# Two attention heads per pass, and later expert weight loads, in a fused attention and mixture-of-experts kernel

## The chip, the cores and the metric

One core of one Trainium2 chip. The metric is device time in microseconds (us). Executions of one kernel agree within about 0.3%, so a per cent is well resolved, except where a run is said to scatter. All runs below gave correct results and count as fast ones.

The engines are PE (matmuls and transposes; its weight loads are listed as PEld), DVE (vector), ACT (activations and copies), POOL (here it mainly issues DMAs) and SP (issues DMAs). PSUM is the memory in which the kernel collects PE's results. A head is one (b, h) pair; a pass of the changed kernel is one turn of its loop, with two heads.

## The reference, cut to what matters

```python
B, H, S, Ns, D = 8, 8, 512, 32, 64            # attention: 64 heads (b, h)
scores = (x @ state.T) / sqrt(D)              # 512 x 32 for each head
xread  = softmax_rows(scores) @ state         # "reads of x":     512 x 64
sread  = softmax_rows(scores.T) @ x           # "reads of state":  32 x 64
x = concatenate([xread, sread])               # 4352 tokens x 512
P = exp(x @ w_gate - max)                     # router logits, 8 experts
for _ in range(8):                            # normalisation (Sinkhorn)
    P /= P.sum(1); P /= P.sum(0); P *= N / E
out = sum(P[:, e:e+1] * (relu(x @ w1[e]) @ w2[e]) for e in range(8))
```

## The kernel before

The attention loop handles one head at a time:

```python
mwp = tile_pool("moe_w", bufs=2); gps = tile_pool("gate_psum", bufs=1, PSUM)
for e in range(E):                       # expert weights, first thing
    nc.gpsimd.dma_start(out=w1e, ...); nc.gpsimd.dma_start(out=w2e, ...)
# ... transposed state stT_all for all heads ...
for bh in range(NH):                     # 64 heads
    nc.sync.dma_start(out=x_nat, in_=x[b, h]...)          # 128 x (4*64), f32
    nc.vector.tensor_copy(out=x_natb, in_=x_nat)          # bf16
    for c in range(4):
        nc.tensor.transpose(xT_ps[:, c, :], x_nat[:, c, :], identf)   # x transposes
    nc.scalar.copy(out=xT, in_=xT_ps)                     # to bf16
    nc.tensor.matmul(esc_ps, sT, xT)                      # scores, 32 x 512
    nc.scalar.activation(out=esc, in_=esc_ps, func=Exp, scale=SCALE, accum_out=rs2)
    for c in range(4): nc.tensor.transpose(eT_ps[:, c, :], esc[:, ts(c, P)], ...)
    nc.vector.tensor_copy(out=eT, in_=eT_ps)
    for c in range(4): nc.tensor.matmul(xr_ps[:, c, :], esc[:, ts(c, P)], s1)   # 65 columns: reads and row sum
    nc.vector.reciprocal(rs1, xr_ps[:, :, D])
    # ... four scalings of 64 columns, two on ACT and two on DVE ...
    for c in range(4): nc.tensor.transpose(xrT_ps[:, c, :], xr[:, c, :], ident)  # read transposes
    for c in range(4): nc.tensor.matmul(sr_ps, eT[:, c, :], x_natb[:, c, :])     # state reads
    # ... scale, transpose, copies into xmT, the transposed tokens ...
for nt in range(34):                     # router logits, 128 tokens each
    # four matmuls of 8 columns into a "gp" PSUM tile, then Exp into Pm
# ... normalisation of Pm on DVE, with one small PE matmul an iteration ...
# ... experts: h = relu(w1.T x), y = w2.T h, acc += Pm * y ...
```

The softmax here doesn't subtract the row's maximum and nothing guards it: scores larger than these inputs give would overflow.

## Time and profile before

| stage (from the timeline) | us |
|---|---|
| until the first scores | 19.4 |
| attention | to 247.9 |
| logits, normalisation, first expert matmuls | to 295 |
| the rest of the experts, output | to 1222.1 |

First the page of the kernel before: span, busy time by engine, then two rows in 40 slices of the span. The digits are tenths, in the first row of busy time and in the second of the clock that was recorded as granted to PE.

```profile
span 1222.1 us, 14811 instructions
PE 1180.9 (97%) x6013; PEld 566.2 (46%) x6104; DVE 337.8 (28%) x804; ACT 472.8 (39%) x1063; POOL 16.2 (1%) x26
...
PE   5999999994999999999999999999999999999998
...
PEclk9999999996999999999999999999999999999999
```

PE is the busy engine. The dip in slice 10 is the normalisation. Groups of instructions of the same kernel follow: line, engine, operation, tiles, shapes, count, then busy us, mean ns of one, idle time before. L114 are x transposes, L152 read transposes, L120 scores, L137 x reads.

```profile
L114 PE MATMUL xT_ps<-identf,x_nat 128*64 128x128 f32 x256 | 83.6, 421 | 11.6 <-DMA x_nat<-in_x_dram 9.6
L152 PE MATMUL xrT_ps<-ident,xr 128*64 128x128 bf16 x256 | 63.7, 312 | 0.5 <-DVE xmT L167 0.3
L120 PE MATMUL esc_ps<-xT,stT_all 64*32 64x512 bf16 x64 | 38.7, 605 | 0.0
L137 PE MATMUL xr_ps<-st_all,esc 32*128 32x65 bf16 x256 | 35.4, 231 | 0.0
```

Matmuls overlap, so these means are latencies. The distance between starts gives PE's real time, and by that measure a head takes 3.56 us (27 heads from 100.4 to 196.6 us). The chain of waits of the kernel before, from 100 to 110 us, is PE alone ("by line" gives shares of the window):

```profile
by line: PE xT_ps L114 34.0%; PE xrT_ps L152 20.3%; PE esc_ps L120 16.1%; PE xr_ps L137 10.4%; PE sr_ps L157 9.8%; PE eT_ps L130 6.5%; PE srT_ps L162 4.8%
```

This is the timeline of PE in the kernel before, where the experts begin: start, us, line, operation, count of matmuls run together.

```profile
250.03 1.01 PE L211 MATMUL h_ps<-xmT,w1e 128*128 128x512 bf16 x2
...
250.99 1.44 PE L211 MATMUL h_ps<-xmT,w1e 128*128 128x512 bf16 x3
...
252.37 1.22 PE L211 MATMUL h_ps<-xmT,w1e 128*128 128x512 bf16 x4
...
254.50 1.02 PE L211 MATMUL h_ps<-xmT,w1e 128*128 128x512 bf16 x4
```

Three 512-column matmuls took 1.44 us at 251 us, and four took 1.02 us at 254.5 us. Within those three the starts lay 0.38 and 0.43 us apart, within the four 0.22 us. PE therefore has two rates here and was at the lower one when attention ended. Scores are also 512 columns wide and took 604 to 606 ns in all 64 heads, against a median of 379 ns in the experts. The Trainium skill, "TensorE: Matmul & The Clock Gate", section "Single matmul latency", gives (219 + N) / 1.2 ns at the low clock and (398 + N) / 2.4 ns at the high one: 609 and 379 for N = 512. This trace agrees with both within 1%, though the page states it for a full array, which these scores (64x32) do not fill. The recorded clock does not show it: it reads 9 or more from the first slice, attention's slices included. The packed trace of this kernel has no clock entry before 252.8 us, where the matmuls get shorter, and the page counts time without an entry as full.

Last, the normalisation in the kernel before: window, its length, then busy us (and instructions) of PE, PEld, DVE, ACT, POOL, the granted clock, the DMA share and GB/s.

```profile
276.00:295.50 19.50, 3.43 (x13) 2.82 (x13) 14.63 (x35) 0.00 (x0) 0.00 (x0) 0.61 0.00 1
```

PE has 3.4 us of work in 19.5 us; DVE works alone.

### The profile page before, as it was taken

The numbers are of one execution on the slowest core, as the hardware profiler recorded it, in microseconds if no ns is written. First come the engines' busy times: TensorE is split into PE (matmuls) and PEld (weight loads), VectorE is DVE, ScalarE is ACT, GpSimd is POOL, SyncE is SP. The second block draws the span as 40 slices with busy tenths as digits, with TensorE's granted clock in tenths as the row PEclk, the third lists the DMA queues.
The fourth block names the chain that finished last, engine by engine and source line by source line (L and its number), as shares of the span: only waits on it lengthen the run. The fifth ranks groups of instructions, "written<-read, shape, count | busy, mean of one in ns | idle before, by whom it ended". The sixth has DMA issues, their size and how long they took to land.

```text
span 1222.1 us, 14811 instructions
## 1 busy us (share of the span) xinstructions
PE 1180.9 (97%) x6013; PEld 566.2 (46%) x6104; DVE 337.8 (28%) x804; ACT 472.8 (39%) x1063; POOL 16.2 (1%) x26
## 2 busy tenths in 40 slices
PE   5999999994999999999999999999999999999998
PEld 3545544542445444544454445444544544454444
DVE  2444443426212122122222112122122222123333
ACT  3555555540333333433333333333433333333332
POOL 2000000000000000000000000000000000000000
PEclk9999999996999999999999999999999999999999
DMA  9211111000001200300040004000400040001112
GB/s 172 56 37 37 39 35 40 14 1 1 1 1 26 44 1 1 56 13 1 1 69 1 1 1 69 1 1 1 69 1 1 1 69 1 1 1 70 69 69 87
DMA packets 53892, 35.31 MB, mean 29 GB/s; under 512 B 37184, under 2 KB 45376, under 8 KB 53824
## 3 DMA queue, kind: packets, MB, share of 16 engines
q0 software_dynamic: 15136, 17.05, 9.6%
q1 hardware_dynamic: 38688, 17.31, 5.1%
q8 instruction: 48, 0.79, 0.3%
q14 instruction: 20, 0.16, 0.1%
HBM read 42.48 MB, written 8.91 MB: 42 GB/s over the span
## 4 chain that ended last, share of the span: by engine, by line
PE 96%; DVE 2%; DMA 1%; issue 1%; ACT 0%; ACTq 0%
PE y_ps L221 38%; PE h_ps L211 38%; PE xT_ps L114 6%; PE xrT_ps L152 4%; PE esc_ps L120 3%; PE xr_ps L137 2%; PE sr_ps L157 2%; DMA x_nat<-in_x_dram 1%; PE eT_ps L130 1%; PE srT_ps L162 1%; DVE ske L186 0%; PE ske_ps L188 0%; PE stT_ps L94 0%; DVE Pm L185 0%; DVE Pm L191 0%
## 5 line engine op out<-in xcount | busy, mean ns | idle before, releaser
L215 ACT ACTIVATE hte<-h_ps 128x512 bf16<-128x512 f32 (+1 forms) x576 | 330.2, 574 | 625.6 <-PE h_ps L211 589.9
L221 PE MATMUL y_ps<-w2e,hte 128*128 128x512 bf16 x2127 | 481.8, 380 | 4.3 <-DVE acc L227 1.6
L211 PE MATMUL h_ps<-xmT,w1e 128*128 128x512 bf16 (+1 forms) x2262 | 482.4, 368 | 2.4 <-issue 0.2
L231 DVE SCALAR_TENSOR_TENSOR acc<-y_ps,Pm,acc 128x512 f32<-128x512 f32 x238 | 178.7, 751 | 628.2 <-PE y_ps L221 627.3
L211 PEld LDWEIGHTS <-w1e 128*128 128x128 bf16 x2304 | 224.5, 98 | 242.7 <-issue 0.6
L221 PEld LDWEIGHTS <-hte 128*128 128x128 bf16 x2176 | 212.9, 98 | 255.6 <-issue 4.7
L114 PE MATMUL xT_ps<-identf,x_nat 128*64 128x128 f32 x256 | 83.6, 421 | 11.6 <-DMA x_nat<-in_x_dram 9.6
L152 PE MATMUL xrT_ps<-ident,xr 128*64 128x128 bf16 x256 | 63.7, 312 | 0.5 <-DVE xmT L167 0.3
L117 ACT CAST xT<-xT_ps 64x512 bf16<-64x512 f32 x64 | 36.7, 574 | 28.9 <-PE xT_ps L114 28.0
L152 PEld LDWEIGHTS <-xr 128*64 128x64 bf16 x256 | 29.5, 139 | 39.2 <-issue 10.6
L227 DVE TENSOR_SCALAR acc<-y_ps,Pm 128x512 f32<-128x512 f32 x34 | 25.3, 750 | 74.7 <-PE y_ps L221 70.2
L114 PEld LDWEIGHTS xT_ps<-identf,x_nat 128*64 128x64 f32 x256 | 30.7, 145 | 28.1 <-issue 10.0
L123 ACT ACTIVATE esc<-esc_ps 32x512 bf16<-32x512 f32 x64 | 37.2, 581 | 14.9 <-PE esc_ps L120 14.8
L167 DVE COPY xmT<-xrT_ps 64x512 bf16<-64x512 bf16 x64 | 26.7, 417 | 58.2 <-PE xrT_ps L152 58.2
L144 ACT ACTIVATE xr<-xr_ps,rs 128x64 bf16<-128x64 f32 x128 | 38.5, 301 | 7.7 <-DVE rs L140 7.2
L120 PE MATMUL esc_ps<-xT,stT_all 64*32 64x512 bf16 x64 | 38.7, 605 | 0.0
L147 DVE TENSOR_SCALAR xr<-xr_ps,rs 128x64 bf16<-128x64 f32 x128 | 34.6, 271 | 14.1 <-ACT xr L144 13.1
L137 PE MATMUL xr_ps<-st_all,esc 32*128 32x65 bf16 x256 | 35.4, 231 | 0.0
L157 PE MATMUL sr_ps<-x_natb,eT 128*32 128x64 bf16 x256 | 27.9, 240 | 0.0
L160 ACT ACTIVATE sr<-sr_ps,r 32x64 bf16<-32x64 f32 x64 | 19.5, 305 | 16.0 <-PE sr_ps L157 15.6
L110 DVE CAST x_natb<-x_nat 128x256 bf16<-128x256 f32 x64 | 18.5, 289 | 19.4 <-PE sr_ps L157 15.1
L169 ACT COPY xmT<-srT_ps 64x32 bf16<-64x32 bf16 x64 | 11.4, 178 | 30.6 <-PE srT_ps L162 30.2
(41 smaller groups left out, 232.4 us busy)
## 6 DMA issues: line engine op xcount, KB each, us to landing
out_dram<-o SPq DMA_DIRECT2D x34, 256.0 KB, 2.0
x_nat<-in_x_dram SPq DMA_DIRECT2D x64, 128.0 KB, 2.2
w1e<-in_moe_w_dram POOLq DMA_DIRECT2D x8, 1024.0 KB, 8.2
w2e<-in_moe_w_dram POOLq DMA_DIRECT2D x8, 1024.0 KB, 10.0
st_all<-in_state_dram POOLq DMA_DIRECT2D x1, 256.0 KB, 7.9
wg<-in_moe_w_gate_dram POOLq DMA_DIRECT2D x1, 8.0 KB, 6.9
```

The source lines that it names most:

```text
L114: nc.tensor.transpose(xT_ps[:, c, :], x_nat[:, c, :], identf)
L117: nc.scalar.copy(out=xT, in_=xT_ps.rearrange("d c p -> d (c p)"))
L120: nc.tensor.matmul(esc_ps, sT, xT, start=True, stop=True)
L123: nc.scalar.activation(out=esc, in_=esc_ps, func=ACT.Exp, scale=SCALE, accum_out=rs2)
L137: nc.tensor.matmul(xr_ps[:, c, :], esc[:, ts(c, P)], s1, start=(c == 0), stop=(c == NCHUNK - 1))
L144: nc.scalar.activation(out=xr[:, c, :], in_=xr_ps[:, c, :D], func=ACT.Copy, scale=rs1[:, c:c + 1])
L152: nc.tensor.transpose(xrT_ps[:, c, :], xr[:, c, :], ident, tile_position=(0, 0))
L157: nc.tensor.matmul(sr_ps, eT[:, c, :], x_natb[:, c, :], start=(c == 0), stop=(c == NCHUNK - 1))
L211: nc.tensor.matmul(h_ps[:, :nn], w1e[:, dc, ts(fc, P)], xmT[:, dc, noff:noff + nn], start=(dc == 0), stop=(dc == DC - 1))
L215: nc.scalar.activation(out=hte[:, fc, :nn], in_=h_ps[:, :nn], func=ACT.Relu)
L221: nc.tensor.matmul(y_ps, hte[:, fc, ts(ns, P)], w2e[:, fc, :], start=(fc == 0), stop=(fc == FC - 1))
L231: nc.vector.scalar_tensor_tensor(acc[:, k, :], y_ps, pvec, acc[:, k, :], op0=ALU.mult, op1=ALU.add)
```

## The change

Its intent: the two heads of a pair go through attention together. Their 64-wide heads fill 128 columns or partitions, with a block-diagonal state (zeros between the heads) keeping them apart. Expert weights are loaded behind the sixth pair's x instead of at the start.

```diff
-    st1_all = singles.tile([Ns, NH, D + 1], BF16)
+    st_all = singles.tile([2 * Ns, NH2, 2, D], BF16)
+    nc.vector.memset(st_all, 0.0)
+    for hl in range(2):
+        nc.gpsimd.dma_start(out=st_all[ds(hl * Ns, Ns), :, hl, :], in_=state_r[:, :, hl, :])
-    for e in range(E):            # weight loads at the start
-        ...
-        for bh in range(NH):
+        for k in range(NH2):      # 32 passes
+            if k == 5:
+                for e in range(E):
+                    ...           # for e < 2: one element of x_nat is copied into w1e and w2e first,
+                    ...           # so that the loads wait for this x
-                nc.tensor.transpose(xT_ps[:, c, :], x_nat[:, c, :], identf)
+                nc.tensor.transpose(xT_ps[:, c, :], x_nat[:, c, :, :], identf)     # both heads
-            nc.tensor.matmul(esc_ps, sT, xT, start=True, stop=True)               # 32 x 512
+            nc.tensor.matmul(esc_ps, stT_all[:, k, :], xT, start=True, stop=True) # 64 x 512
+            nc.vector.tensor_reduce(rs1, eT, axis=AX.X, op=ALU.add)   # row sums, no column of ones
+            nc.vector.tensor_tensor(xr, xr_ps, rs1_b, op=ALU.mult)    # one scaling of 512 columns
-            # (two ACT and two DVE scalings of 64 columns)
     # ... the rest is the same with both heads side by side (cut)
```

The logits, normalisation and experts are the same text; only an index was renamed.

More of the change, by code (lines that the diff above doesn't have):

```diff
@@ L49 @@
     NH = B * H
+    NH2 = NH // 2
     assert NT * P == N
@@ L63 @@
     acc = singles.tile([P, NT, Dm], F32)
-    st1_all = singles.tile([Ns, NH, D + 1], BF16)
-    state_r = state.rearrange("b h j d -> j (b h) d")
-    nc.gpsimd.dma_start(out=st1_all[:, :, :D], in_=state_r)
-    nc.vector.memset(st1_all[:, :, D:D + 1], 1.0)
-    stT_all = singles.tile([D, NH, Ns], BF16)
+    st_all = singles.tile([2 * Ns, NH2, 2, D], BF16)
+    nc.vector.memset(st_all, 0.0)
+    state_r = state.rearrange("b h j d -> j (b h) d").rearrange(
+        "j (k hl) d -> j k hl d", hl=2)
+    for hl in range(2):
+        nc.gpsimd.dma_start(out=st_all[ds(hl * Ns, Ns), :, hl, :],
+                            in_=state_r[:, :, hl, :])
+    stT_all = singles.tile([P, NH2, 2 * Ns], BF16)
     mwp = ctx.enter_context(tc.tile_pool(name="moe_w", bufs=2))
@@ L78 @@
     w2_tiles = [None] * E
-    for e in range(E):
-        w1e = mwp.tile([P, DC, F], BF16, tag="w1e")
-        nc.gpsimd.dma_start(out=w1e, in_=moe_w1[e].rearrange("(c p) f -> p c f", p=P))
-        w2e = mwp.tile([P, FC, Dm], BF16, tag="w2e")
-        nc.gpsimd.dma_start(out=w2e, in_=moe_w2[e].rearrange("(c p) d -> p c d", p=P))
-        w1_tiles[e] = w1e
-        w2_tiles[e] = w2e
     gps = ctx.enter_context(tc.tile_pool(name="gate_psum", bufs=1, space=bass.MemoryType.PSUM))
     GROUP = 16
-    for g in range(NH // GROUP):
-        stT_ps = gps.tile([D, GROUP, Ns], BF16, tag="gp")
+    for g in range(NH2 // GROUP):
+        stT_ps = gps.tile([P, GROUP, 2 * Ns], BF16, tag="gp")
         for i in range(GROUP):
-            bh = g * GROUP + i
-            nc.tensor.transpose(stT_ps[:, i, :], st1_all[:, bh, :D],
-                                ident[:Ns, :Ns])
+            k = g * GROUP + i
+            nc.tensor.transpose(stT_ps[:, i, :], st_all[:, k, :, :],
+                                ident[:2 * Ns, :2 * Ns])
         nc.scalar.copy(out=stT_all[:, ts(g, GROUP), :], in_=stT_ps)
@@ L100 @@
          tc.tile_pool(name="attn_small", bufs=4) as asm:
-        for bh in range(NH):
-            b, h = divmod(bh, H)
-            s1 = st1_all[:, bh, :]
-            sT = stT_all[:, bh, :]
-            x_nat = asb.tile([P, NCHUNK, D], F32, tag="x_nat")
-            nc.sync.dma_start(out=x_nat,
-                              in_=x[b, h].rearrange("(c p) d -> p c d", p=P))
-            x_natb = asb.tile([P, NCHUNK, D], BF16, tag="x_natb")
+        for k in range(NH2):
+            bh0 = 2 * k
+            b = bh0 // H
+            h0 = bh0 % H
+            dch = h0 // 2
+            tok0 = b * SEG
+            x_nat = asb.tile([P, NCHUNK, 2, D], F32, tag="x_nat")
+            for hl in range(2):
+                nc.sync.dma_start(
+                    out=x_nat[:, :, hl, :],
+                    in_=x[b, h0 + hl].rearrange("(c p) d -> p c d", p=P))
+            if k == 5:
+                for e in range(E):
+                    w1e = mwp.tile([P, DC, F], BF16, tag="w1e")
+                    w2e = mwp.tile([P, FC, Dm], BF16, tag="w2e")
+                    if e < 2:
+                        nc.gpsimd.tensor_copy(out=w1e[0:1, 0, 0:1], in_=x_nat[0:1, 0, 1, 0:1])
+                        nc.gpsimd.tensor_copy(out=w2e[0:1, 0, 0:1], in_=x_nat[0:1, 0, 1, 0:1])
+                    nc.gpsimd.dma_start(out=w1e, in_=moe_w1[e].rearrange("(c p) f -> p c f", p=P))
+                    nc.gpsimd.dma_start(out=w2e, in_=moe_w2[e].rearrange("(c p) d -> p c d", p=P))
+                    w1_tiles[e] = w1e
+                    w2_tiles[e] = w2e
+            x_natb = asb.tile([P, NCHUNK, 2, D], BF16, tag="x_natb")
@@ L110 @@
             nc.vector.tensor_copy(out=x_natb, in_=x_nat)
-            xT_ps = aps.tile([D, NCHUNK, P], F32, tag="xT_ps", bufs=1)
+            xT_ps = aps.tile([P, NCHUNK, P], F32, tag="xT_ps", bufs=1)
             for c in range(NCHUNK):
-                nc.tensor.transpose(xT_ps[:, c, :], x_nat[:, c, :],
-                                    identf)
-            xT = asb.tile([D, S], BF16, tag="xT")
-            nc.scalar.copy(out=xT, in_=xT_ps.rearrange("d c p -> d (c p)"))
-            esc_ps = aps.tile([Ns, S], F32, tag="esc_ps", bufs=1)
@@ L120 @@
-            nc.tensor.matmul(esc_ps, sT, xT, start=True, stop=True)
-            esc = asm.tile([Ns, S], BF16, tag="esc")
-            rs2 = asm.tile([Ns, 1], F32, tag="rs2")
-            nc.scalar.activation(out=esc, in_=esc_ps, func=ACT.Exp,
-                                 scale=SCALE, accum_out=rs2)
-            r2 = asm.tile([Ns, 1], F32, tag="r2")
-            nc.vector.reciprocal(r2, rs2)
-            eT_ps = aps.tile([P, NCHUNK, Ns], BF16, tag="eT_ps", bufs=1)
+                nc.tensor.transpose(xT_ps[:, c, :], x_nat[:, c, :, :], identf)
@@ new lines @@
+            xT = asb.tile([P, NCHUNK, P], BF16, tag="xT")
+            nc.scalar.copy(out=xT, in_=xT_ps)
+            esc_ps = aps.tile([2 * Ns, S], F32, tag="esc_ps", bufs=1)
+            nc.tensor.matmul(esc_ps, stT_all[:, k, :], xT, start=True, stop=True)
+            esc = asm.tile([2 * Ns, S], BF16, tag="esc")
+            rs2 = asm.tile([2 * Ns, 1], F32, tag="rs2")
+            nc.scalar.activation(out=esc, in_=esc_ps, func=ACT.Exp, scale=SCALE,
+                                 accum_out=rs2)
@@ L129 @@
+            eT_ps = aps.tile([P, NCHUNK, 2, Ns], BF16, tag="eT_ps", bufs=1)
             for c in range(NCHUNK):
-                nc.tensor.transpose(eT_ps[:, c, :], esc[:, ts(c, P)],
-                                    ident[:Ns, :Ns])
-            eT = asb.tile([P, NCHUNK, Ns], BF16, tag="eT")
+                nc.tensor.transpose(eT_ps[:, c, :, :], esc[:, ts(c, P)],
+                                    ident[:2 * Ns, :2 * Ns])
+            eT = asb.tile([P, NCHUNK, 2, Ns], BF16, tag="eT")
             nc.vector.tensor_copy(out=eT, in_=eT_ps)
-            xr_ps = aps.tile([P, NCHUNK, D + 1], F32, tag="xr_ps", bufs=2)
@@ L136 @@
-            for c in range(NCHUNK):
-                nc.tensor.matmul(xr_ps[:, c, :], esc[:, ts(c, P)], s1,
-                                 start=(c == 0), stop=(c == NCHUNK - 1))
-            rs1 = asm.tile([P, NCHUNK], F32, tag="rs1")
-            nc.vector.reciprocal(rs1, xr_ps[:, :, D])
-            xr = asb.tile([P, NCHUNK, D], BF16, tag="xr")
-            for c in range(NCHUNK):
-                if c % 2 == 0:
-                    nc.scalar.activation(out=xr[:, c, :], in_=xr_ps[:, c, :D],
-                                         func=ACT.Copy, scale=rs1[:, c:c + 1])
-                else:
-                    nc.vector.tensor_scalar(xr[:, c, :], xr_ps[:, c, :D],
-                                            scalar1=rs1[:, c:c + 1], scalar2=None,
-                                            op0=ALU.mult)
@@ L150 @@
-            xrT_ps = aps.tile([D, NCHUNK, P], BF16, tag="xrT_ps", bufs=1)
-            for c in range(NCHUNK):
-                nc.tensor.transpose(xrT_ps[:, c, :], xr[:, c, :], ident,
-                                    tile_position=(0, 0))
-            sr_ps = aps.tile([Ns, D], F32, tag="sr_small", bufs=1)
-            for c in range(NCHUNK):
-                nc.tensor.matmul(sr_ps, eT[:, c, :], x_natb[:, c, :],
-                                 start=(c == 0), stop=(c == NCHUNK - 1))
-            sr = asm.tile([Ns, D], BF16, tag="sr")
@@ L160 @@
-            nc.scalar.activation(out=sr, in_=sr_ps, func=ACT.Copy, scale=r2)
-            srT_ps = aps.tile([D, Ns], BF16, tag="sr_small", bufs=1)
-            nc.tensor.transpose(srT_ps, sr, ident[:Ns, :Ns])
-            prow = (h % 2) * D
-            dch = h // 2
-            tok0 = b * SEG
-            nc.vector.tensor_copy(out=xmT[prow:prow + D, dch, tok0:tok0 + S],
-                                  in_=xrT_ps.rearrange("d c p -> d (c p)"))
-            nc.scalar.copy(out=xmT[prow:prow + D, dch, tok0 + S:tok0 + SEG],
-                           in_=srT_ps)
+            rs1 = asm.tile([P, NCHUNK, 2], F32, tag="rs1")
@@ new lines @@
+            nc.vector.tensor_reduce(rs1, eT, axis=AX.X, op=ALU.add)
+            nc.vector.reciprocal(rs1, rs1)
+            nc.vector.reciprocal(rs2, rs2)
+            xr_ps = aps.tile([P, NCHUNK, 2, D], F32, tag="xr_ps", bufs=2)
+            for c in range(NCHUNK):
+                nc.tensor.matmul(xr_ps[:, c, :, :], esc[:, ts(c, P)],
+                                 st_all[:, k, :, :], start=True, stop=True)
+            xr = asb.tile([P, NCHUNK, 2, D], BF16, tag="xr")
+            rs1_b = _dc.replace(rs1, ap=[rs1.ap[0], rs1.ap[1], rs1.ap[2], [0, D]])
@@ new lines @@
+            nc.vector.tensor_tensor(xr, xr_ps, rs1_b, op=ALU.mult)
+            xrT_ps = aps.tile([P, NCHUNK, P], BF16, tag="xrT_ps", bufs=1)
+            for c in range(NCHUNK):
+                nc.tensor.transpose(xrT_ps[:, c, :], xr[:, c, :, :], ident,
+                                    tile_position=(0, 0))
+            nc.vector.tensor_copy(out=xmT[:, dch, tok0:tok0 + S],
+                                  in_=xrT_ps.rearrange("d c p -> d (c p)"))
+            sr_ps = aps.tile([2 * Ns, 2, D], F32, tag="sr_small", bufs=1)
@@ new lines @@
+            for c in range(NCHUNK):
+                nc.tensor.matmul(sr_ps, eT[:, c, :, :], x_natb[:, c, :, :],
+                                 start=(c == 0), stop=(c == NCHUNK - 1))
+            sr = asm.tile([2 * Ns, 2, D], BF16, tag="sr")
+            nc.scalar.activation(out=sr, in_=sr_ps, func=ACT.Copy, scale=rs2)
+            srT_ps = aps.tile([P, 2, Ns], BF16, tag="sr_small", bufs=1)
+            nc.tensor.transpose(srT_ps, sr, ident[:2 * Ns, :2 * Ns])
+            for hl in range(2):
+                nc.scalar.copy(out=xmT[ds(hl * D, D), dch, tok0 + S:tok0 + SEG],
+                               in_=srT_ps[ds(hl * D, D), hl, :])
@@ L217 @@
                 for ns in range(nn // P):
-                    k = (noff + ns * P) // P
+                    kk = (noff + ns * P) // P
                     y_ps = mps.tile([P, Dm], F32, tag="y_ps")
@@ L224 @@
                                          start=(fc == 0), stop=(fc == FC - 1))
-                    pvec = Pm[:, k, e:e + 1]
+                    pvec = Pm[:, kk, e:e + 1]
                     if e == 0:
-                        nc.vector.tensor_scalar(acc[:, k, :], y_ps,
+                        nc.vector.tensor_scalar(acc[:, kk, :], y_ps,
                                                 scalar1=pvec, scalar2=None,
@@ L230 @@
                     else:
-                        nc.vector.scalar_tensor_tensor(acc[:, k, :], y_ps,
-                                                       pvec, acc[:, k, :],
+                        nc.vector.scalar_tensor_tensor(acc[:, kk, :], y_ps,
+                                                       pvec, acc[:, kk, :],
                                                        op0=ALU.mult, op1=ALU.add)
@@ L236 @@
         out_r = out.rearrange("(k p) d -> p k d", p=P)
-        for k in range(NT):
+        for kk in range(NT):
             o = osb.tile([P, Dm], F32, tag="o")
-            nc.vector.tensor_copy(o, acc[:, k, :])
-            nc.sync.dma_start(out=out_r[:, k, :], in_=o)
+            nc.vector.tensor_copy(o, acc[:, kk, :])
+            nc.sync.dma_start(out=out_r[:, kk, :], in_=o)
 _INS = ['x', 'state', 'moe_w_gate', 'moe_w1', 'moe_w2']
```

## The prediction

> **What bounds the kernel now.** The page gives PE 97% busy of 1222.1 us. The timeline splits the span: attention until about 247 us; router logits and the normalisation, mixed with the first expert, until 295 us; then experts at one 128x512 matmul per 0.216 us (some 940 us in all), which the change does not touch. Only attention counts.
>
> In attention the chain of waits is PE alone, without gaps (100 to 110 us: 34% x transposes, 20% read transposes, 16% scores). Start-to-start times in the timeline give PE 3.53 us a head: x transposes 1.12, read transposes 0.79, scores 0.535, x reads 0.42, state reads 0.36, state-read transpose 0.16, exp transposes 0.15. By the groups table ACT has 2.43 us of work a head, DVE 1.79; neither binds.
>
> The clock row says 0.9 or more, which I do not believe here: a score matmul of 512 columns takes 605 ns against 379 in the experts, and the first expert matmuls start 0.43 us apart until about 252 us, 0.22 after. PE runs attention at half rate. The Trainium skill, "TensorE: Matmul & The Clock Gate", Part 4, says that the full clock does not engage for transposes; this trace agrees. So PE time goes by columns streamed (128 bf16 columns 0.107 us, 128 f32 columns transposed 0.213) plus a weight load of 0.10 to 0.14 us that shows wherever PE switches tile.
>
> **What changes.** Two heads a pass, 32 passes. Transposes of x and of the reads stay four a pass, so their number halves; so do the score matmuls, at the same 512 columns. Read matmuls go from 64 or 65 to 128 columns, exp transposes from 32 to 64: only switches are saved there. Estimates a pass, from the durations above:
> - x transposes 1.25 (a 128-column weight load of some 0.18 us hides under 0.213 within a run; 32 columns took 98 ns, 64 130)
> - read transposes 0.70, scores 0.535, x reads 0.63, state reads 0.57, exp transposes 0.25, state-read transpose 0.16.
> Sum 4.1 us against 7.06 for two heads: 2.96 saved, times 32 = 95 us, all on the chain.
>
> ACT a pass: about 2.05 us (was 4.86). DVE: cast 0.45, exp copy 0.33, new sum 0.4, two reciprocals 0.35, new scaling of 512 PSUM columns 0.7, copy 0.42 = about 2.7 us (was 3.58). Both stay under 4.1; PE remains the limit.
>
> Start: the expert weights now wait for the sixth x tile. Before, PE stood 6.3 us for x behind them (timeline, 10 to 16 us) and scores began at 19.4 us. The new memset of about 4 us delays the state, so I expect scores at about 15 us: 4 gained. The weights then load under the passes; x should be far enough ahead, 0 to 3 us of stalls.
>
> **Predicted time:** 1223 - 95 - 4, less some 2 from fewer switches = 1122 us; 1088 to 1148 should hold it 8 times in 10. Chances: faster by over 2% 0.97, within 2% 0.02, slower 0.01.
>
> **What would show it.** Attention ends near 148 us; scores, x transposes and read transposes halve in count at unchanged means (605, 421, 310 ns); x reads rise from 231 to about 290 ns; PE gapless at 4.1 us a pass; DVE two thirds busy there, ACT half; normalisation gap (20 us) and experts the same, only earlier.
>
> **What would make it wrong.** More non-transpose columns per us could lift the clock: scores of 380 ns, a pass of 3.1 us, 1090 in all. The other way: PE waits for the longer DVE chain (copy, sum, reciprocal, scaling before the read transposes), or transposes are interleaved more, each switch showing a 0.18 us load: 4.8 us a pass, 1145. Weight loads starving x could cost 10 us.

## More of the kernel before

Everything is unrolled in Python, and a scheduler orders each engine's instructions when the program is built. So the order that runs is not the order of the text, and a small edit can change it.

## The result

| | before | after |
|---|---|---|
| median us (range, runs) | 1223.6 (1222.45 to 1225.29, 12) | 1103.54 (1102.53 to 1104.3, 8) |
| ratio, 95% interval | | 0.9018 (0.9009 to 0.9027) |
| first scores at | 19.4 | 15.7 |
| attention ends at | 247.9 | 143.8 |
| from there to the end | 974.2 | 957.7 |

A ratio is the mean time of one kernel's runs over that of the other's runs of the same rounds, so it is not quite the ratio of the medians quoted. Below, "us won" or "lost" against a kernel run in another round is the difference of two such ratios times 1223.6 us.

The time lies inside the predicted range, 18.5 us below the point. The page and the groups of the changed kernel (L126 x transposes, L157 read transposes, L131 scores, L150 x reads):

```profile
span 1101.5 us, 12726 instructions
PE 1070.8 (97%) x5279; PEld 524.7 (48%) x5368; DVE 306.5 (28%) x580; ACT 396.6 (36%) x805; POOL 17.1 (2%) x31
...
PEclk9999999999999999999999999999999999999999
...
L126 PE MATMUL xT_ps<-identf,x_nat 128*128 128x128 f32 x128 | 42.0, 442 | 11.6 <-DMA x_nat<-in_x_dram 9.5
...
L157 PE MATMUL xrT_ps<-ident,xr 128*128 128x128 bf16 x128 | 19.7, 310 | 0.4 <-DVE xr L154 0.4
L131 PE MATMUL esc_ps<-xT,stT_all 128*64 128x512 bf16 x32 | 19.7, 617 | 0.4 <-ACT xT L128 0.3
...
L150 PE MATMUL xr_ps<-st_all,esc 64*128 64x128 bf16 x128 | 19.4, 304 | 0.0
```

Counts halved and means stayed: a transpose or score of two heads costs what one of one head did. Scores still run at the low rate (617 ns). The chain of waits of the changed kernel, from 80 to 90 us, is again nearly all PE ("issue" is time in which PE waited for nothing that the profile shows):

```profile
by line: PE xT_ps L126 35.0%; PE esc_ps L131 17.1%; PE xr_ps L150 16.1%; PE xrT_ps L157 13.9%; PE sr_ps L164 9.9%; PE eT_ps L138 6.5%; PE srT_ps L169 3.2%; PE lg_ps L177 2.7%; issue 0.1%
```

Something stands here that was not there before: L177, the router logits, in the middle of attention. Here is the logits line in both kernels (first the kernel before, then the changed one): least, median and greatest ns, first and last start.

```profile
L175 PE MATMUL lg_ps<-wg,xmT x136: 166/167/214, 30.6 to 267.6; 128*128 128x8 bf16 x136
L177 PE MATMUL lg_ps<-wg,xmT x136: 166/168/214, 25.2 to 149.9; 128*128 128x8 bf16 x136
```

By the traces, 108 of the 136 logits matmuls of the kernel before ran after attention, but only 17 in the changed one. So the normalisation, which needs them all, starts 7 us after attention instead of 21, while PE still has the first expert's work to do. The windows of the changed kernel's normalisation:

```profile
150.50:174.00 23.50, 21.25 (x98) 9.21 (x98) 18.60 (x45) 7.93 (x15) 0.00 (x0) 1.00 0.00 1
174.00:177.00 3.00, 0.39 (x2) 0.32 (x3) 2.42 (x6) 0.00 (x0) 0.00 (x0) 1.00 0.01 3
```

PE is idle for 26.5 - 21.64 = 4.9 us of it, against 16.1 us in the one window of before. That is a gain the prediction did not have.

### The profile page after: what moved, and what is told of

It is laid out like the page before. It is cut to its first block, busy times and chain, and to the rows that moved or that the text cites. A ratio compares the mean times of both kernels' runs of the same rounds, so it can differ in the third digit from the quotient of the medians.

```text
span 1101.5 us, 12726 instructions
## 1 busy us (share of the span) xinstructions
PE 1070.8 (97%) x5279; PEld 524.7 (48%) x5368; DVE 306.5 (28%) x580; ACT 396.6 (36%) x805; POOL 17.1 (2%) x31
## 4 chain that ended last, share of the span: by engine, by line
PE 94%; DVE 2%; DMA 2%; issue 1%; ACT 1%; SPq 0%
PE y_ps L223 42%; PE h_ps L213 41%; PE xT_ps L126 3%; DMA x_nat<-in_x_dram 2%; PE esc_ps L131 1%; PE sr_ps L164 1%; PE xr_ps L150 1%; PE xrT_ps L157 1%; PE eT_ps L138 1%; DVE ske L188 0%; PE lg_ps L177 0%; PE srT_ps L169 0%; DVE Pm L193 0%; DVE Pm L187 0%; DVE sk L184 0%
## 5 line engine op out<-in xcount | busy, mean ns | idle before, releaser
L126 PE MATMUL xT_ps<-identf,x_nat 128*128 128x128 f32 x128 | 42.0, 442 | 11.6 <-DMA x_nat<-in_x_dram 9.5
L126 PEld LDWEIGHTS xT_ps<-identf,x_nat 128*128 128x128 f32 x128 | 21.7, 208 | 24.3 <-issue 13.9
L128 ACT CAST xT<-xT_ps 128x512 bf16<-128x512 f32 x32 | 18.7, 585 | 25.6 <-PE xT_ps L126 25.2
L134 ACT ACTIVATE esc<-esc_ps 64x512 bf16<-64x512 f32 x32 | 18.9, 590 | 19.1 <-PE esc_ps L131 18.9
L154 DVE TENSOR_TENSOR xr<-xr_ps,rs 128x512 bf16<-128x512 f32 x32 | 21.8, 680 | 0.0
L157 PE MATMUL xrT_ps<-ident,xr 128*128 128x128 bf16 x128 | 19.7, 310 | 0.4 <-DVE xr L154 0.4
L131 PE MATMUL esc_ps<-xT,stT_all 128*64 128x512 bf16 x32 | 19.7, 617 | 0.4 <-ACT xT L128 0.3
L164 PE MATMUL sr_ps<-x_natb,eT 128*64 128x128 bf16 x128 | 19.8, 310 | 0.3 <-ACT xmT L171 0.2
L150 PE MATMUL xr_ps<-st_all,esc 64*128 64x128 bf16 x128 | 19.4, 304 | 0.0
L164 PEld LDWEIGHTS <-eT 128*64 128x64 bf16 x128 | 14.4, 160 | 4.8 <-issue 4.0
L177 PEld LDWEIGHTS <-xmT 128*128 128x128 bf16 x136 | 12.7, 127 | 8.0 <-issue 3.8
L157 PEld LDWEIGHTS <-xr 128*128 128x128 bf16 x128 | 14.1, 144 | 3.7 <-issue 2.0
```

Source lines behind the costliest of these rows:

```text
L126: nc.tensor.transpose(xT_ps[:, c, :], x_nat[:, c, :, :], identf)
L131: nc.tensor.matmul(esc_ps, stT_all[:, k, :], xT, start=True, stop=True)
L134: nc.scalar.activation(out=esc, in_=esc_ps, func=ACT.Exp, scale=SCALE, accum_out=rs2)
L150: nc.tensor.matmul(xr_ps[:, c, :, :], esc[:, ts(c, P)], st_all[:, k, :, :], start=True, stop=True)
L154: nc.vector.tensor_tensor(xr, xr_ps, rs1_b, op=ALU.mult)
L157: nc.tensor.transpose(xrT_ps[:, c, :], xr[:, c, :, :], ident, tile_position=(0, 0))
```

## The experiments

Three questions: is the gain PE time in attention, or weights out of the way? What are the earlier logits worth? Why is PE at the low rate, and does its work bind attention? No kernel was refused. All outputs are right.

An edit can also move PE's instructions. By the order of PE's weight loads in the traces, `a_weights_first` and `b_weights_late` keep their parent's order, `a_warm_start` keeps it but for the burst, and `a_logits_last` keeps it through all of attention but for the logits. In the other runs the order in attention changed too, so their totals hold that as well.

### Weight loads, each way

`a_weights_first` is the changed kernel with the old loads; `b_weights_late` is the kernel before with only the late ones. The order of PE's weight loads is identical to its parent's in both.

```diff
# a_weights_first
+    for e in range(E): ...      # weight loads at the start, as before
-            if k == 5: ...
# b_weights_late
-    for e in range(E): ...
+            if bh == 11: ...    # the same block, behind the twelfth head's x
```

> The changed kernel with the expert weights loaded at the start, as the kernel before does; the PE order is the same, instruction for instruction. Main theory (the gain is PE time in attention, halved in columns by pairing): the ratio to the kernel before stays near 0.90, at 1100 to 1112 us; PE stands still for x a few us more at the start and a few us less between 20 and 60 us. Rival (the gain comes from keeping 8 weight transfers out of the way of x): at least 20 us lost, 1124 us or more.

> The kernel before with only the later weight loads (behind the twelfth head's x), the PE order the same. Main theory: 0 to 6 us gained at the start, 1217 to 1223 us. Rival (weight transfers in the way of x were what cost): 1203 us or less.

Measured: `a_weights_first` 1107.85 us, ratio 0.905 (0.9036 to 0.9063), 3.9 us lost. `b_weights_late` 1217.82 us, ratio 0.9951 (0.9936 to 0.9965), 6.0 us won. The rival falls: moving the loads is worth 4 to 6 us, and the rest of the 120 is elsewhere.

### The logits, each way

`b_logits_in` puts each batch's logits into the attention loop of the kernel before. `a_logits_last` holds all logits of the changed kernel back behind attention.

```diff
# b_logits_in
+            if bh % H == H - 1:
+                for nt in range(NT):
+                    if b * SEG < (nt + 1) * P <= (b + 1) * SEG: ...   # the logits of nt
-    for nt in range(NT): ...
# a_logits_last
+    wg2 = gsb.tile([P, DC, E], BF16, tag="wg2")
+    nc.gpsimd.tensor_copy(out=wg2[0:1, 0, 0:1], in_=xmT[0:1, DC - 1, N - 1:N])
+    nc.gpsimd.tensor_copy(out=wg2, in_=wg)
     for nt in range(NT): ...    # reads wg2 in place of wg
```

> The kernel before with the router logits of each batch placed inside the attention loop, no other edit. In the changed kernel most logits ran during attention and PE stood about 7 us in the normalisation, not 20. If that earlier normalisation is worth the part of the gain that the prediction lacked, this kernel gains 12 to 22 us: 1201 to 1211 us. If the position of the logits does not matter because PE does the same work in all: 1220 to 1226 us.

> The changed kernel with all router logits held back behind the last attention result (the gate weights are copied once more, and the copy waits for that result). If the earlier logits give what the prediction lacked: 12 to 22 us lost, 1115 to 1126 us, with PE idle about 20 us in the normalisation again. If not: 1102 to 1107 us.

Measured: `b_logits_in` 1211.28 us, ratio 0.9893 (0.9879 to 0.9908), 13.1 us won. `a_logits_last` 1122.73 us, ratio 0.917 (0.9154 to 0.9185), 18.6 us lost against the changed kernel. Most of the normalisation in windows, first in `b_logits_in`, then in `a_logits_last`:

```profile
258.50:282.00 23.50, 21.34 (x100) 9.23 (x98) 18.63 (x45) 7.91 (x15) 0.00 (x0) 1.00 0.00 1
176.00:195.00 19.00, 3.59 (x12) 3.05 (x13) 13.93 (x34) 0.00 (x0) 0.00 (x0) 0.50 0.00 0
```

Each kernel takes on the other's picture: `b_logits_in` leaves PE 2.2 us idle in 23.5, `a_logits_last` 15.4 us in 19. In `b_logits_in` attention itself ends 4.2 us later than before, at 252.1 us, with the logits in it, and what follows is 16.7 us shorter. In `a_logits_last` it ends at 142.2 us, only 1.6 us earlier than with the logits. The placement is therefore worth about 19 us in the changed kernel. It is no part of the change's text; the scheduler did it.

`a_logits_last` shows one more thing. Its attention has the changed kernel's instructions in the same order, without the logits. Here are 18 passes of each, first the changed kernel, then `a_logits_last`:

```profile
63.66:134.77 71.11, 71.07 (x471) 46.86 (x468) 35.97 (x126) 35.19 (x126) 0.00 (x0) 1.00 0.27 60
63.49:134.47 70.98, 67.82 (x398) 41.73 (x396) 35.99 (x126) 32.88 (x108) 0.00 (x0) 1.00 0.26 60
```

PE had some 0.29 us a pass less to do, yet a pass took 3.94 us in place of 3.95. The time freed became waits of PE, 0.18 us a pass of it as plain gaps; the one wait on another engine that the trace names for PE's matmuls is for ACT's copy of xT, 0.3 us before every second score. So in the changed kernel the logits ran in time that PE would otherwise have waited. PE is full there, but its own work is not all that sets the pass: waits between PE, ACT and DVE do too. Which of them binds was not isolated.

### More work for DVE, more for PE

```diff
# a_dve_more
+            xr2 = asb.tile([P, NCHUNK, 2, D], BF16, tag="xr2")
+            nc.vector.tensor_tensor(xr2, xr_ps, rs1_b, op=ALU.mult)
# a_pe_more: the four read transposes of a pass twice
+            for c in range(NCHUNK):
+                nc.tensor.transpose(xrT_ps[:, c, :], xr[:, c, :, :], ident, tile_position=(0, 0))
```

> The changed kernel with the scaling of the reads done twice by DVE (second copy unused): 32 times 0.68 us, 22 us more DVE work in attention. Main theory (PE binds attention, DVE has about 2.0 us of work in a pass of 3.95): 1102 to 1110 us. Rival (the DVE chain binds): 1120 us or more.

> The changed kernel with the four read transposes of a pass done twice into the same place: 128 more transposes of 128 columns. Main theory (PE binds, 0.107 us for each at half rate, plus a visible weight load now and then): 13 to 20 us lost, 1116 to 1124 us. At the full rate they would cost 7 us, 1110. Rival (PE does not bind): 1107 us or less.

Measured: `a_dve_more` 1116.6 us, ratio 0.9124 (0.911 to 0.9138), 13.0 us lost. This misses both expectations: slower than the main theory said, faster than the rival. A pass went from 3.95 to about 4.35 us, 0.4 of the 0.68 us added, though DVE still has idle time. The changed kernel's attention thus has little slack behind its DVE steps. That fits `a_logits_last`, where a pass did not shorten with 0.29 us less for PE. But 211 of the 736 weight loads in attention, logits left out, stand elsewhere in PE's order, so how much is delay and how much order stays open.

`a_pe_more` was the surprise: 1076.33 us, ratio 0.8817 (0.8769 to 0.8865), with runs from 1073 to 1086. 128 more transposes made it 24.6 us *faster*. The number lies in the range written for the rival ("1107 us or less"), but no theory had a gain in view. The timeline of its scores and of the read transposes before them shows where it happened:

```profile
55.80 0.63 PE L131 MATMUL esc_ps<-xT,stT_all 128*64 128x512 bf16 x1
...
57.49 0.40 PE L157 MATMUL xrT_ps<-ident,xr 128*128 128x128 bf16 x4
57.72 0.39 PE L160 MATMUL xrT_ps<-ident,xr 128*128 128x128 bf16 x4
...
58.70 0.40 PE L131 MATMUL esc_ps<-xT,stT_all 128*64 128x512 bf16 x1
```

From one pass to the next a score fell from 0.63 to 0.40 us, four read transposes from 0.6 to 0.4 us, and all later scores stayed at 0.40. PE had gone to its high rate during attention, and passes then came every 2.6 us, not every 3.95. Transposes were more than half of its PE instructions in a pass, and the only ones added; the edit moved others.

### bf16 transposes, and transposes as plain matmuls

`a_xT_bf16` transposes the bf16 copy of x. `a_plain_T` does likewise and replaces the transposes of x, of the exponentials and of the reads by plain matmuls with the identity.

```diff
# a_xT_bf16
-                nc.tensor.transpose(xT_ps[:, c, :], x_nat[:, c, :, :], identf)       # xT_ps F32
+                nc.tensor.transpose(xT_ps[:, c, :], x_natb[:, c, :, :], ident)       # xT_ps BF16
# a_plain_T
+                nc.tensor.matmul(xT_ps[:, c, :], x_natb[:, c, :, :], ident, start=True, stop=True)
+                nc.tensor.matmul(eT_ps[:, c, :, :], esc[:, ts(c, P)], ident[:2 * Ns, :2 * Ns], ...)
+                nc.tensor.matmul(xrT_ps[:, c, :], xr[:, c, :, :], ident, start=True, stop=True)
#               (xT_ps, eT_ps and xrT_ps are F32)
```

> The changed kernel with the x transposes taken from the bf16 copy of x instead of the f32 tile[...]. Main theory: 128 columns cost 0.107 us in place of 0.213, so 0.43 us a pass and 13 to 16 us in all: 1087 to 1091 us; score matmuls still 605 to 620 ns. If attention is bound elsewhere: 1100 us or more.

> As the last, with the transposes of x, of the exponentials and of the reads done as plain matmuls with the identity into f32 PSUM: the same columns at the same places, but no transpose mode. If transposes keep the clock at half (main theory): score matmuls fall to about 380 ns, PE time of a pass nearly halves, and the time falls under 1070 us, limited then by DVE and ACT. Rival (the half rate is from short instructions and waits, whatever their kind): scores stay at 605 to 620 ns, 1087 to 1100 us, with some loss to dearer copies from f32 PSUM.

Measured: `a_xT_bf16` 1090.84 us, ratio 0.8915 (0.8902 to 0.8929), 12.6 us won, close to the 13 to 16 expected: a pass took 3.59 us in place of 3.95, with 0.5 us less for the x transposes, so PE's columns are on the path (the order changed as well). `a_plain_T` 1092.22 us, ratio 0.8927 (0.8914 to 0.894), in the rival's range. Its scores:

```profile
L132 PE MATMUL esc_ps<-xT,stT_all x32: 582/633/636, 13.8 to 126.1; 128*64 128x512 bf16 x32
```

No score left the low rate, with nearly all transposes gone. So the prediction's reason for the low rate, transposes not counting as activity, falls. PE had gaps of 0.22 us a pass here, so this run alone could leave it to the gaps; but in `a_pe_more` PE did rise, with more transposes. Together they say: the kind of instruction did not decide.

### Raising the rate on purpose

New theory: attention stays at the low rate because no stretch of it is dense enough to raise it, and a raised rate persists while PE stays dense. The test is a burst of useless matmuls: in pass 14 of the changed kernel (`a_warm_mid`), before its first pass (`a_warm_start`), in head 28 of the kernel before (`b_warm_mid`), and in pass 14 of the bf16 variant (`x_warm_mid`).

```diff
# a_warm_mid (x_warm_mid: 32 times, on a_xT_bf16)
+            if k == 14:
+                wu_ps = gps.tile([P, S], F32, tag="gp")
+                for _ in range(20):
+                    nc.tensor.matmul(wu_ps, ident, x_natb, start=True, stop=True)
# a_warm_start: 20 times with stT_all[:, 0:8, :], ahead of the loop
# b_warm_mid: if bh == 28, 60 times with x_natb (256 columns)
```

> The changed kernel with 20 useless 128x512 matmuls in pass 14 (about 60 us), their result unused. New theory: PE has two rates; attention stays at the half rate because no stretch of it is dense enough to raise it, whatever the kind of matmul, and once raised the rate stays. Then score matmuls fall from about 615 to about 400 ns at the burst and stay there, a pass falls from 3.95 to about 2.6 us, and the time is 1075 to 1090 us in spite of the burst's 4 to 8 us. Rival (the rate follows the momentary mix; the run with doubled transposes was fast for its order): 1107 to 1112 us.

> The same burst before the first pass, once the transposed state is there (about 16 us). New theory: at most 1065 us if the raised rate outlasts the waits for x between 20 and 45 us; if those waits (2 to 3 us each) lower it again, 1100 to 1112 us with scores fast only at first. Rival: 1107 to 1112 us.

> The kernel before with 60 useless 128x256 matmuls in head 28 (about 110 us). New theory: scores fall from 605 to about 390 ns from there on, a head from 3.53 us to some 2.6 us (ACT has 2.43 us of work), 30 us won less a burst of 7 to 13: 1200 to 1212 us. Rival: 1230 to 1237 us.

> The kernel with bf16 x transposes (1091 us) with 32 useless 128x512 matmuls in pass 14. New theory: scores at about 400 ns after it and 1070 to 1084 us; DVE and ACT bind then, so that it gains less than the changed kernel does. Rival: 1096 to 1102 us.

Measured:

| run | us | ratio (95%) | scores |
|---|---|---|---|
| a_warm_mid | 1089.47 | 0.8905 (0.8889 to 0.8921) | 0.38 us from the burst to the end |
| a_warm_start | 1104.25 | 0.9024 (0.901 to 0.9037) | 0.40 us for five passes, then 0.63 |
| b_warm_mid | 1229.47 | 1.0047 (1.0032 to 1.0061) | about 0.38 us for three heads, then 0.61 |
| x_warm_mid | 1091.87 | 0.8919 (0.8904 to 0.8934) | 0.38 to 0.40 us for six passes, then about 0.63 |

`a_warm_mid` is as the theory expected: 13.8 us won, 20 useless matmuls included. `a_warm_start` is its second branch, as these windows show (burst at 16 to 23 us):

```profile
23.00:33.00 10.00, 8.80 (x92) 5.75 (x91) 8.34 (x28) 7.36 (x25) 0.00 (x0) 1.00 1.17 204
33.00:38.00 5.00, 0.35 (x2) 0.38 (x3) 0.00 (x0) 0.00 (x0) 0.00 (x0) 0.63 1.22 196
38.00:60.00 22.00, 21.43 (x143) 13.79 (x141) 11.23 (x39) 10.27 (x36) 0.00 (x0) 0.50 0.32 72
```

PE waited 5.6 us for x at 32 us and came back at the low rate. The recorded clock reads 0.50 here, from 38 to 60 us. In the changed kernel it reads full at the same pace and score duration, 0.63 us. So the record follows the rate once the rate has changed, and is read as full before that, whatever the rate.

`b_warm_mid` and `x_warm_mid` missed both theories: the rate rose and did not last. These are windows of `b_warm_mid` after its burst:

```profile
129.00:135.00 6.00, 5.47 (x55) 3.47 (x53) 1.98 (x10) 3.40 (x13) 0.00 (x0) 1.00 0.16 37
135.00:140.00 5.00, 5.00 (x34) 2.53 (x34) 2.69 (x12) 3.23 (x13) 0.00 (x0) 0.51 0.15 34
```

The scheduler had spread 22 of the 60 matmuls among other work, where the rate stayed low; the record has the rise at 128.3 us, within the run of 38 that began at 124.2 us. It fell at about 135 us with no longer wait on PE than 0.46 us since the burst. So persistence takes more than the absence of long waits. How dense PE must be was not measured; the orders of these kernels differ too, so the total of `b_warm_mid` is not a price of the burst alone. Its logits had moved into attention, as in `b_logits_in` (17 left after it, not 108), and the rest was 17.7 us shorter; yet attention ended 22.8 us later than before, at 270.7 us, with heads of 4.0 us after the burst against 3.55 before it. Why they were longer was not found. "Dense enough" is a name for what was seen, not a rule shown.

## Why the prediction was right

The time fell within its range, by a mechanism that was mostly the one given, with three terms off. It took the span of before after attention (974.2 us) as fixed and attention's end as 148.

- **PE binds attention, by columns streamed at the low rate: right in the main, too simple for the changed kernel.** PE was busy for 100 of 100 us in the kernel before, counts halved at unchanged means (605 to 617, 312 to 310, 421 to 442 ns), and `a_xT_bf16` won 12.6 us with fewer columns. But in `a_logits_last` 0.29 us less for PE did not shorten a pass, and in `a_dve_more` 0.68 us more for DVE lengthened it by 0.4, with DVE only half busy in the changed kernel (two thirds expected). Waits between the engines limit the pass about as tightly as PE's own work.
- **The step "transposes do not count, hence half rate": the half rate was right, its reason wrong.** `a_plain_T` has almost no transposes and the same rate; `a_pe_more` has more of them and rose. The reason did not enter the sum, so it did no harm to the number. But the prediction tied a rise to "more non-transpose columns", and `a_pe_more` rose with more transposes only.
- **The term "4.1 us a pass": PE's work was 0.4 less, the pass only 0.15 less.** Distances between starts over 18 passes without waits for x (63.7 to 134.8 us): x transposes 1.04 us a pass (1.25 expected), read transposes 0.56 (0.70), scores 0.47 (0.535), x reads 0.53 (0.63), state reads 0.55 (0.57), exp transposes 0.36 (0.25), state-read transpose 0.16. That is 3.67 us. There were fewer switches between tiles than expected: read transposes always ran four together in these passes. The logits took 0.29 us more, which makes the 3.95; but without them a pass took 3.94, so PE's work alone did not set it. Attention ended at 143.8 us, 4 before the 148 expected.
- **The start: right.** Scores began at 15.7 us (15 expected), though the memset took 1.77 us, not 4. Waits for x after the first came to 5.4 us (9.5 less the 4.1 before the first tile), above the 0 to 3 expected. Late loads won 3.9 us in the changed kernel.
- **The term "normalisation gap the same": wrong, and the largest error.** From the end of attention to the end of the span took 957.7 us, not 974.2: 16.5 us less. In the normalisation PE stood idle for 4.1 us, not 16.1. `a_logits_last` puts a price of 18.6 us on the logits' place by itself.

Ledger of the spans, 1222.1 - 1101.5 = 120.6 us: start 3.7, attention from first score to end 228.5 - 128.1 = 100.4, the rest 16.5. With the logits held back, the total (1122.7 us) is the 1122 of the prediction; that is partly luck, as the pass was shorter than expected and what followed attention longer (978.6 us).

Left open: why the scheduler moved the logits in one kernel and not in the other (the text gives no reason, and `b_weights_late`, with 108 logits matmuls after attention, shows that late loads alone do not do it), which waits set the pass beside PE's work, the share of order in `a_dve_more`, and the exact condition under which PE's rate rises or lasts. `a_pe_more` was the fastest kernel run, faster than both, but by a rise whose moment was not fixed on purpose; its four runs lie 12.6 us apart. `a_xT_bf16` gives 12.6 us within 1.1 us, for one changed line and a tile type. The combination of bf16 transposes with a rate that lasts was tried once (`x_warm_mid`) and did not hold.

## What to carry to other kernels

Read PE's rate from the duration of one known matmul shape in each stage, not from busy time or the recorded clock; here a stage that was 100% busy ran at half rate, so a column there took twice the time that it took in the experts. Pairing narrow heads so that one 128-wide transpose or 512-column matmul serves two of them took PE's work for two heads from 7.1 to 3.67 us here. A busy engine is not yet the only bound: without the logits PE had less to do and a pass took as long, and more work for a half-busy DVE cost 13 us. A change in one stage may move instructions of the next: compare where each group first and last starts before crediting the change itself.

## What the Trainium skill lacked or had wrong

- "TensorE: Matmul & The Clock Gate", Part 4, says the high clock does not engage for transposes. Here a run with 128 more transposes went to it and stayed (scores 633 to 403 ns), and one with plain matmuls in their place did not (median 633 ns).
- The same page, "What's actually happening", says that the clock is high after one busy window of about 3.4 us. PE was 100.00 us busy of 100 in the kernel before and did not rise in 228 us of attention. What counts as busy is lacking; it is not the busy time of the records.
- The same table has the clock fall after an idle window of about 3.4 us. In `a_warm_start` the fall came with a wait of 5.6 us, though by the record (0.63 over 33 to 38 us) at 34.3 us, 2.3 us into it. In `b_warm_mid` it fell about 5 us after the burst with no wait over 0.46 us, which the page's idle window does not cover.
- The same page, "Seeing it yourself", warns that the clock's trace events are unreliable. One form of it can be named: before the first change of rate in a run the packed trace has no entry, and the views here print 1.00 whatever the rate is (scores of 633 ns at 1.00 in the changed kernel, at 0.50 in `a_warm_start`).
